# Row maxima of an attention kernel transposed in fp32 and split on GpSimd, and two of four row blocks normalized on ScalarE

## The chip, the cores and the metric

The kernel runs on one core of one Trainium2 chip. The time is the device time of one execution in microseconds, and the time given is the median of the runs. A profiled execution has two figures: its own time, as the runs have it, and its span, from the first to the last instruction of the program.

## The reference, cut to what matters

One transformer block over S = 2048 rows of width D = 512. A condition vector gives six modulation rows. The first half is attention with 32 heads of width 16 that share one key and one value head; the second half is a gated feed-forward layer with F = 1792.

```python
def _A_ref(x, wq, wk, wv, wo):
    q = (x @ wq).reshape(B, S, H, Dh).transpose(0, 2, 1, 3)
    k = x @ wk
    v = x @ wv
    scores = einsum("bhqd,bkd->bhqk", q, k) * (Dh ** -0.5)
    p = softmax(scores, axis=-1)
    o = einsum("bhqk,bkd->bhqd", p, v)
    return o.transpose(0, 2, 1, 3).reshape(B, S, H * Dh) @ wo

def _B_ref(x, w_gate, w_up, w_down):
    return (sigmoid(x @ w_gate) * (x @ w_up)) @ w_down

sa, ca, ga, sb, cb, gb = (silu(c) @ w_mod).reshape(6, -1)
h = layernorm(x) * (1 + ca) + sa
x = x + ga * _A_ref(h, ...)
h = layernorm(x) * (1 + cb) + sb
x = x + gb * _B_ref(h, ...)
```

The weights are drawn large, so the scores are large, and softmax needs the maximum of each row before the exponential is taken.

## The kernel before, in words

**Maxima first, then scores.** The rows are cut into 4 blocks of 512, and a block's 32 heads into 8 units of 4 heads: 32 units in all. For a unit the kernel computes its scores twice. First with queries on the partitions: a matmul writes 128 queries by 512 keys into a PSUM bank (`sa`), and VectorE takes the maximum of each row out of it (`mx`, one TENSOR_REDUCE a bank, 64 banks a unit, 2048 in all). Then with keys on the partitions (`st`): ScalarE takes the exponential (`P`), and TensorE multiplies it with the values (`c`). The products are fp16 with high and low parts in the contraction; P, V and their product are fp32.

**How the maximum gets into the scores.** The second product subtracts the maximum by itself: the query tile `qp` (fp16, 64 rows of contraction for each of two row groups) has two rows that hold the maximum divided by 16, its high and its low fp16 part, and the key tile `kp` has -16 there. So after a unit's 64 maxima `max_end` (line 547) reduces them to `m16` (128x16), makes the two parts on VectorE (`mhl`), and `max_rows` (line 555) turns them on TensorE with an fp16 identity into a PSUM bank of the `sa` rotation, ScalarE copies that to `mh`, and SyncE's queue issues four small DMAs that put the rows into `qp` (line 564). The first `st` of the unit waits for these DMAs.

**The main loop** (line 968) has 512 steps, 16 a unit. A step issues four `st` with their exponentials, four `sa` with their maxima, which run `A0` banks ahead of the step's own unit, and the value product of two steps ago. Blocks 1 to 3 carry in the same steps, in pieces between the score matmuls, the output projection and the feed-forward layer of the block before (`po`, `pgu`, `pd`); block 0 carries the queries' projection of later blocks (`pq`). With A0 = 80 the last maxima of unit i fall into step 16i-5, `max_end` and `max_rows` into step 16i-4; the unit's first `st` is in step 16i. From step 492 on no maxima are left. The last block's output projection and feed-forward layer follow the loop.

**What sets the order.** TensorE, VectorE and ScalarE run in the order in which the code is written (`Ordered`, line 122) up to the end of the loop; GpSimd's and SyncE's instructions outside `pool1` and `sp1` are put in order by the scheduler's own clock. Each engine's queue runs strictly in that order. Ahead of the loop the order is written out by hand in `PLAN` (line 36), a string of tokens: S statistics of a 128-row tile, ra rb rc the inverse deviation (VectorE, GpSimd, VectorE), N the normalization of a tile (`ln_norm`, line 389), T the transposes of a block, H E L the high part, full value and low part of the modulated rows, pk KB KL the keys, pv V the values, q QA QL the queries' projection, pm me pr m the modulation, `a` one `sa` matmul, `x` its maximum, mx and my `max_end` and `max_rows` of unit 0. `PLAN` has A0 tokens `a`. Beside this GpSimd splits the weights into fp16 parts during block 0 (`wst`, `gw`, `wdh`, `wdl`).

Of the kernel before, what the change touches and what calls it, by code (L numbers as in the profile page):

```python
# [8 lines left out]
F16 = mybir.dt.float16  # L9
F32 = mybir.dt.float32  # L10
AF = mybir.ActivationFunctionType
ALU = mybir.AluOpType
# [4 lines left out]
P = 128  # L17
# [14 lines left out]
SM = 16.0  # L32
# [1 line left out]


PLAN = (
# [12 lines left out]
)  # L49

H32 = ('ADAD', 'AAAA', 'AAAA', 'AAAA')
HLO = ('PDPD', 'PPPP', 'PPPP', 'PPPP')

A0 = 80
LAG = 2


# [21 lines left out]
def adaln_mqa_glu_kernel(  # L79
# [15 lines left out]
    pool, sp = nc.gpsimd, nc.sync  # L95
# [3 lines left out]
    x = x[0]  # L99
    out = out[0]  # L100

    cp = ctx.enter_context(tc.tile_pool(name="cp", bufs=1))
    wp = ctx.enter_context(tc.tile_pool(name="wp", bufs=1))
# [11 lines left out]
    def sbank(name):  # L115
        return psum["s"].tile([P, 512], F32, tag=name, name=name, bufs=psum["banks"][name])
# [14 lines left out]
    pe, dve, act = Ordered(nc.tensor), Ordered(nc.vector), Ordered(nc.scalar)  # L131
# [51 lines left out]

    ident = cp.tile([P, P], F32, name="ident")
    make_identity(nc, ident)
    ident16 = cp.tile([P, P], F16, name="ident16")
    pool.tensor_scalar(ident16, ident, 1.0, 0.0, op0=ALU.mult, op1=ALU.add)
    mhalf = cp.tile([P, 1], F32, name="mhalf")
    pool.memset(mhalf, -0.5)

# [169 lines left out]
    def xs(b):  # L360
        return [xall[:, 4 * b + t, :] for t in range(4)]
# [21 lines left out]
    def ln_newton(b):  # L383
        mv, ve, rs, nw = lns[b]
        dve.tensor_tensor(nw, rs, rs, op=ALU.mult)
        dve.scalar_tensor_tensor(nw, nw, -0.5, ve, op0=ALU.mult, op1=ALU.mult)
        dve.scalar_tensor_tensor(rs, nw, 1.5, rs, op0=ALU.add, op1=ALU.mult)

    def ln_norm(b, t):
        mv, ve, rs, nw = lns[b]  # L390
        dve.tensor_scalar(xs(b)[t], xs(b)[t], mv[:, t, 0:1], rs[:, t:t + 1], op0=ALU.subtract, op1=ALU.mult)

    def ln1_tr(b, k):
        pts[b, k] = pt = bank("pt")
# [120 lines left out]
    def get_q(i):  # L515
        b, u = units[i]
        o = u // 2
        if (b, o) not in qps:
            assert (b, o) in qdone
            load_q(b, o)  # L520
        return qps[b, o], 2 * (u % 2)
# [24 lines left out]

    def max_end(i):
        m16 = wp.tile([P, 16], F32, tag="m16", name="m16", bufs=4)
        mhl = wp.tile([P, 2, 16], F16, tag="mhl", name="mhl", bufs=4)
        dve.tensor_reduce(m16.rearrange("p (h t) -> p h t", t=4), mxs[i], axis=AX.X, op=ALU.max)  # L550
        dve.tensor_scalar(mhl[:, 0], m16, 1.0 / SM, None, op0=ALU.mult)
        dve.scalar_tensor_tensor(mhl[:, 1], m16, 1.0 / SM, mhl[:, 0], op0=ALU.mult, op1=ALU.subtract)
        return lambda: max_rows(i, mhl)

    def max_rows(i, mhl):
        qp, pr0 = get_q(i)
        pm = sbank("sa")
        pe.matmul(pm[:32, :P], mhl.rearrange("p h m -> p (h m)"), ident16, start=True, stop=True)
        mh = wp.tile([32, P], F16, tag="mh", name="mh", bufs=4)
        act.activation(mh, pm[:32, :P], AF.Identity)  # L560
        for j in range(2):
            for h in range(2):
                r = 64 * j + 48 + h
                sp.dma_start(qp[r:r + 1, pr0:pr0 + 2, :], mh[16 * h + 8 * j:16 * h + 8 * j + 8, :])


    def st_tile(i, t, pr, j):
# [287 lines left out]
    def q_end(b, o):  # L855
# [3 lines left out]
    blanks.append(blank(pool1))  # L859

    stages = {"S": ln_stats, "ra": ln_eps, "rb": ln_pow, "rc": ln_newton, "N": ln_norm, "T": ln1_tr, "H": ln1_high,
              "E": ln1_full, "L": ln1_low, "pk": k_product, "KB": k_high, "KL": k_end, "pv": v_product, "V": v_end,
              "wh": wq_high, "wl": wq_low, "q": q_part, "QA": q_end, "QL": lambda b, o: q_low(b, o, *q2s.pop((b, o))),
              "pm": mod_product, "me": mod_copy, "pr": mod_sum, "m": mod_end,
              "a": a_next, "x": lambda: a_max(*held.pop(0)), "mx": lambda: rows.append(max_end(0)), "my": lambda: rows.pop()(),
              "lw": load_wq, "lx": load_x, "lm": lambda i: load_mod(i, sp1), "bl": lambda: blanks.append(blank(pool1))}
    for tok in PLAN.split():
        name = tok.rstrip("0123456789")
        stages[name](*[int(z) for z in tok[len(name):]])
    assert not held and apos == A0  # L870
    first.clear()
# [18 lines left out]
    nw, wdone = len(wjobs), 0  # L890
# [77 lines left out]
    for i, (b, u) in enumerate(units):  # L968
# [4 lines left out]
        for kb in range(NKB):  # L973
# [3 lines left out]
            for z in [z for z in waits if z[0] <= s]:  # L977
                waits.remove(z)
                z[1]()
            rows = [max_end(*z) for z in late]  # L980
            an = A0 + 4 * s

# [88 lines left out]
```

## Time and profile before

| what | value |
|---|---|
| median of 3 runs (lowest to highest) | 1727.74 us (1721.31 to 1727.91) |
| the profiled execution's own time | 1730.16 us |
| its span | 1728.4 us |
| first `st` of the loop, from the span's start | 104.62 us |
| first `st` of unit 8 (block 1) | 438.72 us |
| last exponential's score matmul | 1579.99 us |

How it is read: times are in microseconds from the span's start. PE is TensorE's matmuls, PEld its weight loads, DVE VectorE, ACT ScalarE, POOL GpSimd, SP SyncE, whose queue issues the DMAs. A row of a timeline gives the start, the duration, the engine, the line, the operation, what it writes and reads, how many were merged, and in brackets how long the engine had been idle before it and what ended that. A row of windows gives for a stretch the busy time of each engine and the granted TensorE clock (1.00 is full). A row of the chain gives the start and the time that one link holds on the path that ended last. Most matmuls are listed under the line of a helper (L128).

### The profile page before, as it was taken

Reading aid. Unit: us, or ns where it says so; the run is one execution under the profiler, and the core shown is the slowest. Engines: PE = TensorE matmul, PEld = TensorE weight load, DVE = VectorE, ACT = ScalarE, POOL = GpSimd, SP = SyncE. Lnnn points to the kernel's source line nnn. Section 1 sums busy time; section 2 is a strip of 40 time slices with the busy share of each in tenths; the row PEclk is TensorE's granted clock in tenths of the full one; section 3 lists DMA queues with packets and bytes.
Section 4 is the critical chain, followed back from the end, with each engine's and each line's share of the span. In section 5 each row is a group of like instructions: output and inputs, shape, how many; then the busy total and the mean of one; then the engine's idle time right before and its main releaser. Section 6 shows DMA issues by size and latency. Waiting matters only on the chain.

```text
span 1728.4 us, 34828 instructions
## 1 busy us (share of the span) xinstructions
PE 1690.8 (98%) x13968; PEld 576.7 (33%) x13968; DVE 1441.5 (83%) x2424; ACT 1234.2 (71%) x2254; POOL 590.7 (34%) x659
## 2 busy tenths in 40 slices
PE   6999999999999999999999999999999999999998
PEld 3323323333333333333323333333333333323443
DVE  8899999999998998998899898898898888932311
ACT  4358888888888777777778777777778777774100
POOL 4341453542454131332254231223254130231533
PEclk9999999999999999999999999999999999999999
DMA  7121322320101010111011110111001110011211
GB/s 241 45 89 35 118 89 75 129 80 23 58 23 45 30 50 11 38 47 35 24 41 32 41 57 5 33 41 50 32 28 46 32 54 5 30 50 55 76 59 49
DMA packets 66282, 90.88 MB, mean 53 GB/s; under 512 B 14800, under 2 KB 41424, under 8 KB 66120
## 3 DMA queue, kind: packets, MB, share of 16 engines
q1 hardware_dynamic: 66120, 88.66, 16.2%
q8 instruction: 109, 1.79, 0.4%
q14 instruction: 53, 0.43, 0.1%
HBM read 67.68 MB, written 16.22 MB: 49 GB/s over the span
## 4 chain that ended last, share of the span: by engine, by line
PE 81%; DVE 14%; ACT 2%; issue 1%; DMA 1%; POOL 0%; SPq 0%; POOLq 0%; DVEq 0%; ACTq 0%
PE c L128 25%; PE st L128 19%; PE pgu L128 12%; DVE mx L128 11%; PE sa L128 8%; PE pd L128 5%; PE pgu L152 4%; PE pd L152 2%; ACT P L128 2%; PE po L128 2%; PE pq L128 2%; PE pt L128 1%; DVE st L128 1%; DMA xall<-in_A_x_dram 1%; PE po L152 1%
## 5 line engine op out<-in xcount | busy, mean ns | idle before, releaser
L128 DVE TENSOR_REDUCE mx<-sa 128x1 f32<-128x512 f32 x2048 | 1288.1, 684 | 113.6 <-PE sa L128 107.1
L128 ACT ACTIVATE P<-st 128x512 f32<-128x512 f32 x2048 | 1136.6, 596 | 288.3 <-PE sa L128 246.5
L128 PE MATMUL sa<-kp,qp 64*128 64x512 f16 x2048 | 748.2, 383 | 6.8 <-DVE mx L128 6.2
L128 PE MATMUL st<-qp,kp 64*128 64x512 f16 x2048 | 747.6, 380 | 5.9 <-ACT P L128 2.5
L128 PE MATMUL c<-P,V 128*32 128x512 f32 (+1 forms) x5296 | 577.9, 509 | 0.9 <-ACT cs L128 0.2
L128 PEld LDWEIGHTS <-kp 64*128 64x128 f16 x2048 | 177.2, 94 | 516.5 <-issue 427.9
L128 PE MATMUL pgu<-h2h,gw 64*128 64x512 f16 x1344 | 247.1, 376 | 0.3 <-DVE ot L128 0.2
L128 PEld LDWEIGHTS <-qp 64*128 64x128 f16 x2048 | 186.8, 93 | 167.8 <-issue 77.3
L128 PEld LDWEIGHTS c<-P,V 128*32 128x32 f32 x5296 | 104.5, 108 | 191.4 <-issue 182.5
L791 POOL TENSOR_SCALAR th<-th 128x512 f32<-128x512 f32 x42 | 25.9, 617 | 384.1 <-ACT th L128 384.1
L128 PE MATMUL pgu<-h2l,gw 64*128 64x512 f16 x672 | 134.7, 376 | 0.0
L128 PEld LDWEIGHTS <-gw 64*128 64x128 f16 x2016 | 101.0, 94 | 84.5 <-issue 7.4
L501 POOL MEMSET qp<- 32x2048 f16 x28 | 50.3, 1798 | 64.3 <-issue 32.1
L814 POOL TENSOR_TENSOR ot<-ot,gb 128x512 f32<-128x512 f32 x10 | 12.7, 1269 | 168.8 <-ACT ot L128 168.8
L152 PE MATMUL pgu<-h2h,gw 128*128 128x512 f16 x224 | 67.0, 379 | 1.2 <-POOL h2h L307 1.2
L276 POOL TENSOR_SCALAR wst<-wst 128x512 f32<-128x512 f32 x46 | 28.4, 618 | 114.0 <-DMA wst<-in_B_w_gate_dram 57.4
L797 POOL TENSOR_TENSOR gl<-th,gh 128x512 f16<-128x512 f32 x56 | 64.8, 1157 | 4.7
L785 ACT ACTIVATE th<-pgu 128x512 f32<-128x512 f32 x14 | 8.4, 597 | 79.3 <-PE pgu L152 79.3
L794 DVE SCALAR_TENSOR_TENSOR th<-th,pgu 128x512 f32<-128x512 f32 x14 | 9.6, 688 | 66.0 <-PE pgu L152 51.9
L128 DVE COPY u<-pgu 128x512 f32<-128x512 f32 x42 | 28.5, 680 | 37.9 <-PE st L128 22.0
L654 POOL TENSOR_TENSOR raw<-raw,rb 128x512 f32<-128x512 f32 x15 | 19.1, 1274 | 105.3 <-DMA rb<-lD 73.2
L792 POOL TENSOR_TENSOR th<-th,u 128x512 f32<-128x512 f32 x42 | 53.3, 1268 | 5.3 <-DVE u L128 2.3
(156 smaller groups left out, 1304.6 us busy)
## 6 DMA issues: line engine op xcount, KB each, us to landing
gw<-wD SPq DMA_DIRECT2D x56, 512.0 KB
wD<-gw SPq DMA_DIRECT2D x14, 512.0 KB
wm<-in_w_mod_dram SPq DMA_DIRECT2D x6, 1024.0 KB
qp<-qD SPq DMA_DIRECT2D x96, 64.0 KB
qD<-q SPq DMA_DIRECT2D x16, 256.0 KB
raw<-cs SPq DMA_DIRECT2D x128, 32.0 KB
xr<-in_A_x_dram SPq DMA_DIRECT2D x16, 256.0 KB
out_dram<-ot SPq DMA_DIRECT2D x16, 256.0 KB
```

What stands on the lines that cost most here:

```text
L128: return (lambda *a, **k: keep(f_(*a, **k))) if pinned else f_
L152: pe.matmul(self.bank, l_, r_, start=(n == 0), stop=(n == self.n - 1))
L276: pool.tensor_scalar(w_, w_, SW, 0.0, op0=ALU.mult, op1=ALU.add)
L501: eng.memset(qp[j:j + 32], 0.0)
L654: keep(pool.tensor_tensor(raw, raw, rb, op=ALU.mult))
L785: act.activation(th, p_, AF.Tanh, scale=0.5 / (SH * SW))
L791: pool.tensor_scalar(th, th, 1.0, 1.0, op0=ALU.add, op1=ALU.mult)
L792: pool.tensor_tensor(th, th, u_, op=ALU.mult)
L794: dve.scalar_tensor_tensor(th, th, 1.0, p_, op0=ALU.add, op1=ALU.mult)
L797: pool.tensor_tensor(lo, th, hi, op=ALU.subtract)
L814: pool.tensor_tensor(ot, ot, mods[5], op=ALU.mult)
```

## The change

Three things are edited, and the written order is made anew.

- **Maxima.** `max_end` makes `m16` alone. `max_rows` turns `m16` (fp32, 128x16) with the fp32 identity, ScalarE copies the result, scaled by 1/16, to `m32` (16x128, fp32), and GpSimd makes the high part (TENSOR_SCALAR) and the low part (TENSOR_TENSOR) in `mh` (16x2x128, fp16). These two and the four DMAs are put into the scheduler's order with priority. The fp16 identity is gone.
- **Normalization.** For blocks 2 and 3 of the rows `ln_newton` makes -mean times the inverse deviation as well (one more VectorE instruction of 128x4), and the eight tiles are normalized by ScalarE's ACTIVATE with scale and bias in place of VectorE's TENSOR_SCALAR.
- **Lead.** A0 goes from 80 to 84: `max_end` of unit i falls into step 16i-5, and no maxima are left from step 491 on.

```diff
@@ PLAN: two of its lines, before and after @@
-    'S12 wl0 T01 S13 T02 m0 E01 H00 T03 ra1 E00 S20 rb1 H01 E03 H02 S21 L00 E02 L01 q000 H03 rc1 L02 N10 q001 L03 '
+    'T00 m0 S12 T01 H00 S13 E00 T02 E01 H01 L00 T03 ra1 S20 H02 E02 L01 rb1 q000 H03 E03 pk00 L02 rc1 q001 L03 pk01 '
...
-    'q113 x a x a QA11 x a x a QL11 x a x x x '
+    'q101 x QL03 a q102 x a x q103 x a a QA10 q110 x a q111 x QL10 a x a q112 mx x a my q113 x a x QA11 a x a x a '
+    'QL11 x a x a x a x a x a x a x a x a x a x a x a x a x x x '
@@
-A0 = 80
+A0 = 84
@@
-    ident16 = cp.tile([P, P], F16, name="ident16")
-    pool.tensor_scalar(ident16, ident, 1.0, 0.0, op0=ALU.mult, op1=ALU.add)
@@ ln_newton
+        if b > 1:
+            dve.scalar_tensor_tensor(nw, mv[:, :, 0], -1.0, rs, op0=ALU.mult, op1=ALU.mult)
@@ ln_norm
-        dve.tensor_scalar(xs(b)[t], xs(b)[t], mv[:, t, 0:1], rs[:, t:t + 1], op0=ALU.subtract, op1=ALU.mult)
+        if b < 2:
+            dve.tensor_scalar(xs(b)[t], xs(b)[t], mv[:, t, 0:1], rs[:, t:t + 1], op0=ALU.subtract, op1=ALU.mult)
+        else:
+            act.activation(xs(b)[t], xs(b)[t], AF.Identity, scale=rs[:, t:t + 1], bias=nw[:, t:t + 1])
@@ max_end
-        mhl = wp.tile([P, 2, 16], F16, tag="mhl", name="mhl", bufs=4)
         dve.tensor_reduce(m16.rearrange("p (h t) -> p h t", t=4), mxs[i], axis=AX.X, op=ALU.max)
-        dve.tensor_scalar(mhl[:, 0], m16, 1.0 / SM, None, op0=ALU.mult)
-        dve.scalar_tensor_tensor(mhl[:, 1], m16, 1.0 / SM, mhl[:, 0], op0=ALU.mult, op1=ALU.subtract)
-        return lambda: max_rows(i, mhl)
+        return lambda: max_rows(i, m16)
@@ max_rows
-        pe.matmul(pm[:32, :P], mhl.rearrange("p h m -> p (h m)"), ident16, start=True, stop=True)
-        mh = wp.tile([32, P], F16, tag="mh", name="mh", bufs=4)
-        act.activation(mh, pm[:32, :P], AF.Identity)
-        for j in range(2):
-            for h in range(2):
-                r = 64 * j + 48 + h
-                sp.dma_start(qp[r:r + 1, pr0:pr0 + 2, :], mh[16 * h + 8 * j:16 * h + 8 * j + 8, :])
+        pe.matmul(pm[:16, :P], m16, ident, start=True, stop=True)
+        m32 = wp.tile([16, P], F32, tag="m32", name="m32", bufs=4)
+        act.activation(m32, pm[:16, :P], AF.Identity, scale=1.0 / SM)
+        mh = wp.tile([16, 2, P], F16, tag="mh", name="mh", bufs=4)
+        with tc.high_priority():
+            pool.tensor_scalar(mh[:, 0], m32, 1.0, 0.0, op0=ALU.mult, op1=ALU.add)
+            pool.tensor_tensor(mh[:, 1], m32, mh[:, 0], op=ALU.subtract)
+            for j in range(2):
+                for h in range(2):
+                    r = 64 * j + 48 + h
+                    sp.dma_start(qp[r:r + 1, pr0:pr0 + 2, :], mh[8 * j:8 * j + 8, h, :])
```

VectorE ahead of the loop, from the statistics of the last tiles to its first maxima (`xall` is the row tile that is normalized in place, `nw` and `rs` the steps to the inverse deviation, `kp` the keys). Before:

```order
L128 TENSOR_TENSOR nw<-rs 128x4
L128 SCALAR_TENSOR_TENSOR nw<-nw,ve 128x4
L128 SCALAR_TENSOR_TENSOR rs<-nw,rs 128x4
L128 TENSOR_REDUCE mx<-sa 128x1 x4
L128 TENSOR_SCALAR xall<-xall,mv,rs 128x512 x4
L128 SCALAR_TENSOR_TENSOR kp<-pk,kh 128x512
L128 TENSOR_REDUCE mx<-sa 128x1 x8
```

After:

```order
L128 TENSOR_TENSOR nw<-rs 128x4
L128 SCALAR_TENSOR_TENSOR nw<-nw,ve 128x4
L128 SCALAR_TENSOR_TENSOR rs<-nw,rs 128x4
L128 SCALAR_TENSOR_TENSOR nw<-mv,rs 128x4
L128 TENSOR_REDUCE mx<-sa 128x1 x4
L128 SCALAR_TENSOR_TENSOR kp<-pk,kh 128x512
L128 TENSOR_REDUCE mx<-sa 128x1 x11
```

The four normalizations of block 3 have left VectorE (those of block 2, a little earlier, as well), and one small instruction has come. On ScalarE seven of the eight now stand in a row:

```order
L128 ACTIVATE h1h_436<-pt,sa,ca 128x512
L128 ACTIVATE h_439<-pt,sa,ca 128x512
L128 ACTIVATE xall<-xall,nw,rs 128x512 x7
L128 ACTIVATE h1h_502<-pt,sa,ca 128x512
L128 ACTIVATE kh<-pk,kbias,kscale 128x512
```

They stand between the rows of block 1 (`h1h`, `h`) and those of block 2, where before the first followed on the second.

SyncE's queue in block 0, around the rows of unit 5 (`qD` is the queries' way through memory, `wst` a weight tile that comes in, `wD` one that goes out, `raw` and `lD` the end of a unit). Before:

```order
L483 DMA qD<-q_4178 128x2x512
L275 DMA wst<-in_B_w_up_dram 128x4x128
L483 DMA qD<-q_4184 128x2x512
L564 DMA qp<-mh 1x8x128 x4
L683 DMA wD<-gw 128x2048
```

After:

```order
L486 DMA qD<-q_4202 128x2x512
L568 DMA qp<-mh 1x8x128 x4
L273 DMA wst<-in_B_w_up_dram 128x4x128
L486 DMA qD<-q_4208 128x2x512
L687 DMA wD<-gw 128x2048
```

The four small DMAs now stand ahead of one weight load and one store of queries.

More of the change, by code (lines that the diff above doesn't have):

```diff
@@ L548, in max_end, with max_rows @@
         m16 = wp.tile([P, 16], F32, tag="m16", name="m16", bufs=4)
-        mhl = wp.tile([P, 2, 16], F16, tag="mhl", name="mhl", bufs=4)
         dve.tensor_reduce(m16.rearrange("p (h t) -> p h t", t=4), mxs[i], axis=AX.X, op=ALU.max)
-        dve.tensor_scalar(mhl[:, 0], m16, 1.0 / SM, None, op0=ALU.mult)
-        dve.scalar_tensor_tensor(mhl[:, 1], m16, 1.0 / SM, mhl[:, 0], op0=ALU.mult, op1=ALU.subtract)
-        return lambda: max_rows(i, mhl)
-    def max_rows(i, mhl):
+        return lambda: max_rows(i, m16)
+    def max_rows(i, m16):
         qp, pr0 = get_q(i)
         pm = sbank("sa")
-        pe.matmul(pm[:32, :P], mhl.rearrange("p h m -> p (h m)"), ident16, start=True, stop=True)
-        mh = wp.tile([32, P], F16, tag="mh", name="mh", bufs=4)
-        act.activation(mh, pm[:32, :P], AF.Identity)
-        for j in range(2):
-            for h in range(2):
-                r = 64 * j + 48 + h
-                sp.dma_start(qp[r:r + 1, pr0:pr0 + 2, :], mh[16 * h + 8 * j:16 * h + 8 * j + 8, :])
+        pe.matmul(pm[:16, :P], m16, ident, start=True, stop=True)
[9 more added lines that the diff above has]
+                    sp.dma_start(qp[r:r + 1, pr0:pr0 + 2, :], mh[8 * j:8 * j + 8, h, :])
     def st_tile(i, t, pr, j):
```

19 rows, old and new, of the table PLAN are left out of this document.

## The prediction

> **What bounds the kernel now.** I read first the totals, then the windows of three stages, then the chain and the timelines inside them. Totals and windows (columns of the latter: stretch, its length, busy time of PE, PEld, DVE, ACT, POOL with instruction counts, granted clock, DMA share, GB/s):
>
> ```profile
> PE 1690.8 (98%) x13968; PEld 576.7 (33%) x13968; DVE 1441.5 (83%) x2424; ACT 1234.2 (71%) x2254; POOL 590.7 (34%) x659
> ```
>
> ```profile
> 0.00:104.62 104.62, 85.12 (x541) 35.83 (x542) 91.02 (x173) 41.95 (x68) 39.83 (x52) 0.93 0.41 135
> 105.00:438.70 333.70, 325.76 (x3287) 103.34 (x3284) 324.61 (x543) 288.08 (x537) 139.93 (x166) 0.98 0.25 80
> 527.70:1488.20 960.50, 959.08 (x7990) 318.28 (x7988) 865.54 (x1438) 745.20 (x1359) 291.84 (x307) 1.00 0.12 35
> 104.62:112.30 7.68, 6.11 (x29) 1.76 (x30) 7.68 (x14) 5.48 (x10) 6.72 (x10) 0.66 0.62 202
> ```
>
> The average (PE 98%) hides three stages. Ahead of the loop DVE works 91.02 of 104.62 us. In block 0 (105 to 438.7) it works 324.61 of 333.70 and idles 9.1; PE's 325.76 is as much, but there PE's in-order queue stands behind DVE's, as the next fence shows. In blocks 1 to 3 PE is full (959.08 of 960.50) and DVE has a tenth free. So an instruction taken from DVE is worth its length ahead of the loop and in block 0, and little later.
>
> **Edit 1, normalization on ScalarE.** The chain ahead of the loop (start, time on the path, link), from two stretches of it:
>
> ```profile
> 35.65 2.76 DVE xall L128 x4
> ...
> 42.81 1.08 DVE rs L128
> ...
> 46.29 3.50 DVE xall L128 x4
> ...
> 101.27 0.32 PE sa L128 x2
> 101.59 0.75 PE pq L128 x3
> ```
>
> Up to 50 us the path runs through DVE, and the eight normalizations of blocks 2 and 3 are links of it: 2.76 + 3.50 = 6.3 us go. Two instructions of 128x4 come (`nw` from mean and inverse deviation). Their nearest row is the link `rs`, 1.08, beside a busy GpSimd; the same kind of work took a fifth of that elsewhere, as the 128x16 instructions below do. I take 0.6 each, 1.2 (ends 0.3 and 2.2). ScalarE takes eight ACTIVATEs; the nearest is
>
> ```profile
> 52.65 0.78 ACT L128 ACTIVATE h1h<-pt,sa,ca 128x512 f16<-128x512 f32 x1 [3.33 <-PE pt L128]
> ```
>
> 0.78 each, 6.2 us at most. ScalarE is busy 41.95 of these 104.62 us, and just there it waits 3.33 us for transposes: that is the cover, so nothing is added. If it fails, block 2's transposes come late by up to the seven in a row, 5.5 us, and the gain is gone.
>
> **Edit 2, four more maxima ahead of the loop.** Four reductions at 0.6 are 2.4 us of DVE more here. They buy nothing by their number (each step of block 0 still has four) but give the rows of a unit one step more to arrive. On the path PE holds the later part (0.75 for three `pq`, 0.32 for one or two `sa`), so four `sa` cost at most 1.3 there, inside DVE's 2.4.
>
> Unit 0's `mhl` pair goes too, 0.3. Sum ahead of the loop: -6.3 + 1.2 + 2.4 - 0.3 = **-3.0**. Ends: -6 (the four reductions fill gaps that DVE has anyhow) and +2.4 (PE holds the start and DVE's gain is lost).
>
> The last lines of the new plan are `x a` pairs with nothing else on PE: DVE paces them, and PE is mostly idle. The window 104.62 to 112.30 shows what that does now: granted clock 0.66, but DVE busy 7.68 of 7.68, so it cost nothing there. I take 0, ends 0 and +2. The Trainium skill's page "TensorE: Matmul & The Clock Gate" (What's actually happening) says that the array falls to half its clock after an idle window of about 3.4 us and recovers after a busy one. By that rule the longer tail would start the loop cold for longer, and the sum would be 2 us higher.
>
> **Edit 3, the maxima's two parts off DVE: block 0.** DVE around unit 1's `max_end`, then unit 3's:
>
> ```profile
> 124.76 12.35 DVE L128 TENSOR_REDUCE mx<-sa 128x1 f32<-128x512 f32 x20
> 137.14 0.22 DVE L128 TENSOR_REDUCE m<-mx 128x16 f32<-128x64 f32 x1
> 137.40 0.17 DVE L128 TENSOR_SCALAR mhl<-m 128x16 f16<-128x16 f32 x1
> 137.60 0.18 DVE L128 SCALAR_TENSOR_TENSOR mhl<-m,mhl 128x16 f16<-128x16 f32 x1
> 137.70 2.48 DVE L128 TENSOR_REDUCE mx<-sa 128x1 f32<-128x512 f32 x4
> 140.37 7.52 DVE L128 TENSOR_REDUCE mx<-sa 128x1 f32<-128x512 f32 x12 [0.19 <-PE sa L128]
> ```
>
> ```profile
> 219.31 0.98 DVE L128 TENSOR_SCALAR mhl<-m 128x16 f16<-128x16 f32 x1
> 220.33 0.54 DVE L128 SCALAR_TENSOR_TENSOR mhl<-m,mhl 128x16 f16<-128x16 f32 x1
> 220.80 2.47 DVE L128 TENSOR_REDUCE mx<-sa 128x1 f32<-128x512 f32 x4
> 223.60 0.69 DVE L128 TENSOR_REDUCE mx<-sa 128x1 f32<-128x512 f32 x1 [0.33 <-PE sa L128]
> ...
> 226.01 7.67 DVE L128 TENSOR_REDUCE mx<-sa 128x1 f32<-128x512 f32 x12 [0.86 <-PE sa L128]
> ```
>
> A step is 4 x 12.35 / 20 = 2.47 us, all DVE. `max_end` holds the next maximum from 137.14 to 137.70; without `mhl` it would start at 137.40, 0.30 sooner. The 0.19 of idle time behind is the PE that could turn only what `mhl` had finished; it goes too. 0.49 for each of the eight units 1 to 8 that block 0 prepares: -3.9. Unit 3's pair took 1.49 to the next maximum where 0.30 is usual, and 0.33 + 0.86 of idle time followed: 1.2 + 1.0 more, -2.2.
>
> The rows' DMAs are late once, at unit 5 (SP's queue, DVE behind it, and the link of the last DMA in the chain):
>
> ```profile
> 311.88 0.36 SPq L483 DMA_DIRECT2D qD<-q  x1
> 312.29 2.71 SPq L564 DMA_DIRECT2D qp<-mh  x4
> ```
>
> ```profile
> 315.28 0.69 DVE L128 TENSOR_REDUCE mx<-sa 128x1 f32<-128x512 f32 x1 [0.89 <-PE sa L128]
> 316.55 0.69 DVE L128 TENSOR_REDUCE mx<-sa 128x1 f32<-128x512 f32 x1 [0.58 <-PE sa L128]
> ```
>
> ```profile
> 314.36 1.68 DMA qp<-mh
> ```
>
> They stood behind a store of queries; the new order has them ahead of it. Of 0.89 + 0.58 I count -1.0.
>
> Against this stands the longer way of the rows. For unit 1 the queue issued them from 138.39:
>
> ```profile
> 138.39 2.71 SPq L564 DMA_DIRECT2D qp<-mh  x4
> ```
>
> so `m` to the last issue takes 1.25 + 2.1, and 1.68 to its landing: 5.0 us of the four steps, 9.9, that stand between `m` and the unit's first scores. New are two GpSimd instructions of 128 elements. Their nearest rows are one of a single element and the 512-element subtractions:
>
> ```profile
> L295 POOL TENSOR_TENSOR nw<-nw,ve x10: 189/190/190, 501.9 to 1277.0; 128x1 f32<-128x1 f32 x10
> ```
>
> ```profile
> 387.21 0.22 DVE L128 TENSOR_REDUCE m<-mx 128x16 f32<-128x64 f32 x1
> ```
>
> ```profile
> 391.98 2.27 POOL L278 TENSOR_TENSOR wdl<-wst,wdh 128x512 f16<-128x512 f32 x2
> ```
>
> 0.19 and 1.13 each; a quarter of the way gives some 0.4, with the hand-over 0.9 for both (ends 0.5 and 2.4). The five steps of the new lead are 12.3, so 12.3 - 5.9 = 6.4 us remain for GpSimd's queue. In the new order the `wdl` pair stands ahead of unit 7's two instructions, and it ended at 394.25. Unit 7's `m`, one step sooner, is at 384.7; its rows would land at 394.25 + 0.9 + 2.1 + 1.68 = 398.9, 1.8 behind 387.21 + 9.9. I count +1.0 for this one unit; elsewhere the queue is clear by then. Block 0: -3.9 - 2.2 - 1.0 + 1.0 = **-6.1**, ends -9.1 (all of DVE's idle time) and +3.
>
> **Edit 3 in blocks 1 to 3.** PE around unit 20's turn of the maxima:
>
> ```profile
> 994.67 1.07 PE L128 MATMUL c<-P,V 128*32 128x512 f32 x8
> 995.55 0.22 PE L128 MATMUL sa<-ident,mhl 128*32 128x128 f16 x1
> 995.70 0.39 PE L128 MATMUL st<-qp,kp 64*128 64x512 f16 x1
> 995.86 0.37 PE L128 MATMUL sa<-kp,qp 64*128 64x512 f16 x1
> ...
> 998.11 1.06 PE L128 MATMUL c<-P,V 128*32 128x512 f32 x8
> 999.11 0.39 PE L128 MATMUL st<-qp,kp 64*128 64x512 f16 x1
> 999.11 0.39 PE L128 MATMUL sa<-kp,qp 64*128 64x512 f16 x1
> ```
>
> After `c` the next `st` and `sa` start together 1.00 later; here 1.03 and 1.19. In fp32, `c` needs 1.00 for 512 columns, so 128 need 0.25 where the fp16 turn held PE for 0.15: +0.1, with a slower weight load +0.2. Against it `sa` was 0.16 late because its bank waited for DVE, which is now 0.30 sooner. Over the 23 units 9 to 31: +2.3 to +4.6 and -3.7; I take **0**, ends -4 and +5. The ACTIVATE out of the bank stays one instruction for one.
>
> **Sum.** -3.0 - 6.1 = -9.1 against the profiled execution's own 1730.2 (span 1728.4): 1721. That execution is 2.4 above the median of the runs, 1727.7; from the median it would be 1718.6. I say 1719.
>
> **Rivals.**
> *The rows come too late (slower).* GpSimd's queue is in order; if what the new order puts ahead of the two instructions waits for a weight load, the first scores of a unit wait, and PE with them. For: GpSimd is busy 139.93 us of block 0, and unit 7 is already over the line. Against: 6.4 us of room, and priority in the order. It decides where the queue holds a unit by more than 6.4 us: three us beyond that at each of the eight units of block 0 cost 24, so 1721 - 7 + 24 = 1738, or 1736 from the median. The Trainium skill speaks for it on its page "GPSIMD Engine Reference" (When to use GPSIMD): elementwise work belongs on VectorE, since GpSimd is about twice as slow with two inputs. No row here shows the 16x128 form.
> *It nets out (no change).* PE holds the start of the loop (+1 ahead of it), block 0 gains only the 0.30 for eight units (-2.4), and the fp32 turn costs its 0.2 for 23 units (+4.6): +3, so 1733 and 1731 from the median. For: the chain after 50 us is PE's. Against: the 0.19 and 0.86 of idle time behind `mhl`.
> *All of it.* Both lower ends, -6 and -9, and -2 later: 1713 and 1711 from the median.
>
> **How the numbers follow.** 0.6 for the forecast (1714 to 1724), 0.22 for no net change, 0.12 for late rows, 0.06 for all of it. The range 1710 to 1730 leaves out the late rows and the upper half of the second. Half a per cent, 8.6 us, is about what a measurement of this kernel tells from no change: below 1719.1 is faster. The forecast lies on that edge. I put 0.42 of its 0.6 below it, because the idle time of DVE that I left out of block 0 (9.1 us in all, of which the rows above use 4) can only shrink, and add all of the last case: 0.48. Slower is the late rows, 0.12; the rest is 0.40.
>
> **What would show it.** Right: the first `st` near 101.6 though 84 maxima are made; `m` directly followed by `mx` and 0.26 between them at all units; unit 8's first `st` near 429.6; steps with `max_rows` in blocks 1 to 3 as long as before. Wrong: ScalarE the longest link between 30 and 55 us; PE or its weight loads waiting for `qp` rows at more than one or two units; GpSimd's two instructions starting many us after ScalarE's copy; a granted clock of half beyond 115 us; a first `st` at 105 or later.

## The result and the profile after

The changed kernel takes 1717.72 us (median), and the kernel before 1726.49 in the six runs that belong to this result (1727.74 is the median of the first three of them): the ratio is 0.9952, with a 95% interval of 0.9939 to 0.9965. Against further runs of the kernel before on another occasion it was 0.9942 (0.9924 to 0.9960). The profile below is of an execution from that second occasion, because the first one that was profiled was disturbed (4015.82 us, where the others took 1716.82 to 1718.80).

Totals of the changed kernel, then windows of its three stages (columns as in the prediction's windows): ahead of the first `st`, block 0 up to unit 8's first `st`, and units 8 to 30:

```profile
PE 1680.2 (98%) x14000; PEld 577.0 (34%) x14000; DVE 1421.9 (83%) x2354; ACT 1237.8 (72%) x2262; POOL 613.1 (36%) x722
```

```profile
0.00:100.71 100.71, 82.71 (x546) 36.15 (x547) 85.33 (x169) 47.16 (x76) 43.91 (x58) 0.97 0.45 151
100.71:428.11 327.40, 320.93 (x3299) 104.26 (x3298) 320.76 (x527) 287.00 (x537) 142.17 (x178) 0.99 0.24 78
428.11:1520.76 1092.65, 1090.48 (x9156) 360.11 (x9153) 974.44 (x1589) 855.43 (x1564) 363.88 (x422) 1.00 0.11 35
```

The last two of these stages in the kernel before:

```profile
104.62:438.72 334.10, 326.16 (x3289) 103.54 (x3289) 325.01 (x543) 288.10 (x537) 140.33 (x166) 0.98 0.25 80
438.72:1535.00 1096.28, 1093.45 (x9137) 360.95 (x9134) 984.17 (x1639) 855.95 (x1564) 347.52 (x377) 1.00 0.12 35
```

All three stages became shorter: by 3.9 us ahead of the loop, 6.7 in block 0 and 3.6 in units 8 to 30, 14.2 in all. That is more than the medians differ, since these two executions lie on opposite sides of their medians. The table has the same split for every kernel below; the last stage (unit 31 and the tail) is 193.4 us in all of them. The stages are differences of `st` start times. Two executions of the kernel before differ by 1.54 us in the first column, 0.99 in block 0 and 0.22 in units 8 to 30; the last section shows where the first two come from.

| kernel | first `st` | block 0 | units 8 to 30 | median | ratio to before (95%) |
|---|---|---|---|---|---|
| before | 104.62 | 334.10 | 1096.28 | 1727.74 | |
| before, another execution | 103.08 | 333.11 | 1096.06 | 1727.43 (one run) | |
| after | 100.71 | 327.40 | 1092.65 | 1717.89 | 0.9942 (0.9924 to 0.9960) |
| before + edit of the maxima | 104.95 | 333.36 | 1093.42 | 1727.05 | 0.9986 (0.9973 to 0.9999) |
| before + ScalarE normalization | 105.34 | 335.20 | 1096.08 | 1728.64 | 1.0000 (0.9989 to 1.0012) |
| before + early projections | 105.09 | 332.60 | 1096.19 | 1729.84 | 1.0019 (1.0009 to 1.0029) |
| after, old way of the maxima | 102.34 | 330.31 | 1095.17 | 1722.82 | 0.9969 (0.9958 to 0.9981) |
| the same, fp16 turn twice | 102.29 | 331.33 | 1095.59 | 1723.26 | 0.9972 (0.9962 to 0.9982) |
| after, normalization on VectorE | 101.05 | 328.09 | 1092.64 | 1717.80 | 0.9944 (0.9927 to 0.9962) |
| after, 80 maxima ahead | 98.41 | 334.84 | 1093.44 | 1721.99 | 0.9970 (0.9957 to 0.9982) |
| after, late projections | 105.53 | 328.72 | 1092.77 | 1721.56 | 0.9965 (0.9951 to 0.9979) |
| after, fp32 turn twice | 102.62 | 327.60 | 1097.55 | 1722.95 | 0.9973 (0.9961 to 0.9984) |
| after, units 2 and 7 old way | 102.68 | 328.07 | 1092.72 | 1717.98 | 0.9940 (0.9926 to 0.9954) |

### The profile page after: what moved, and what is told of

Read it like the earlier page. It is cut to its first block, busy times and chain, and to the rows that moved or that the text cites. A ratio compares the mean times of both kernels' runs of the same rounds, so it can differ in the third digit from the quotient of the medians.

```text
span 4014.0 us, 34893 instructions
## 1 busy us (share of the span) xinstructions
PE 3996.8 (100%) x14000; PEld 798.1 (20%) x14000; DVE 1537.6 (38%) x2354; ACT 1334.3 (33%) x2262; POOL 612.6 (15%) x722
## 4 chain that ended last, share of the span: by engine, by line
PE 99%; issue 0%; DVE 0%; DMA 0%; ACT 0%; POOL 0%; SPq 0%; POOLq 0%; DVEq 0%
PE c L128 30%; PE st L128 16%; PE pgu L128 15%; PE sa L128 14%; PE pd L128 6%; PE pgu L152 5%; PE pd L152 3%; PE pq L128 3%; PE po L128 2%; PE pt L128 1%; PE po L152 1%; PE pk L128 1%; PE pmod L128 0%; PE prow L128 0%; DVE mx L128 0%
## 5 line engine op out<-in xcount | busy, mean ns | idle before, releaser
L128 DVE TENSOR_REDUCE mx<-sa 128x1 f32<-128x512 f32 x2048 | 1393.2, 691 | 1915.9 <-PE sa L128 1455.9
L128 PE MATMUL st<-qp,kp 64*128 64x512 f16 x2048 | 1510.1, 770 | 0.2
L128 PE MATMUL sa<-kp,qp 64*128 64x512 f16 x2048 | 1490.3, 768 | 1.0 <-DVE mx L128 0.8
L128 PE MATMUL c<-P,V 128*32 128x512 f32 (+1 forms) x5296 | 1270.2, 1060 | 0.0
L128 PE MATMUL pgu<-h2h,gw 64*128 64x512 f16 x1344 | 546.9, 830 | 0.0
L128 PE MATMUL pgu<-h2l,gw 64*128 64x512 f16 x672 | 294.5, 832 | 0.0
L128 PE MATMUL pd<-wdh,gl 64*128 64x512 f16 x280 | 118.6, 836 | 0.0
L128 PE MATMUL pd<-wdl,gh 64*128 64x512 f16 x280 | 117.5, 832 | 0.0
L128 PE MATMUL pd<-wdh,gh 64*128 64x512 f16 x280 | 117.2, 830 | 0.0
L152 PE MATMUL pgu<-h2l,gw 128*128 128x512 f16 x112 | 93.6, 836 | 0.0
```

Source lines behind the costliest of these rows:

```text
L128: return (lambda *a, **k: keep(f_(*a, **k))) if pinned else f_
L152: pe.matmul(self.bank, l_, r_, start=(n == 0), stop=(n == self.n - 1))
```

## Experiments

My theory was that of the prediction: VectorE's time ahead of the loop and in block 0 pays, blocks 1 to 3 give nothing. The rivals: PE holds the start of the loop whatever VectorE does; the rows' longer way makes PE wait; the gain lies later than I put it.

### The changed kernel and the kernel before, once more

Edit: none.

> The changed kernel once more, to have a profile that can be set beside the one before. My theory (gain ahead of the loop and in block 0, nothing later): first st near 101.6, unit 8's first st near 429.6, blocks 1 to 3 as long as before, ratio 0.995. Rival A (PE holds the start of the loop): first st at 104 to 106, and block 0 shorter by 8 us or more. Rival B (the gain is in blocks 1 to 3, where max_end frees the banks sooner): first st and unit 8 less than 3 us sooner, the rest shorter by 4 us or more.

> The kernel before once more, for a second profile: how far two executions of the same kernel differ by stage. First st within 1.5 us of 104.62, block 0 within 2 us of 334.1, the rest within 1.5 us of 1289.7.

Measured: the rows and the table above. The first `st` and unit 8 stand near where the theory has them (100.71 and 428.11), and yet units 8 to 30 are 3.6 us shorter, which it excluded. Rival B named that place, but it also forecast less than 3 us in the stages ahead, which gained 10.6. The two executions of the kernel before differ by 0.22 us in units 8 to 30, and no execution has a granted clock under 1.00 there, so these 3.6 are no chance. The first `st` of the second execution, 1.54 sooner, lies just outside the 1.5 expected.

### One edit alone: ScalarE normalization, in the old order and out of the new

```diff
@@ ln_newton and ln_norm, into the kernel before @@
+        if b > 1:
+            dve.scalar_tensor_tensor(nw, mv[:, :, 0], -1.0, rs, op0=ALU.mult, op1=ALU.mult)
...
+        if b < 2:
+            dve.tensor_scalar(xs(b)[t], ...)
+        else:
+            act.activation(xs(b)[t], xs(b)[t], AF.Identity, scale=rs[:, t:t + 1], bias=nw[:, t:t + 1])
```

> The kernel before with the normalization of blocks 2 and 3 on ScalarE and nothing else, in the old order. By the prediction's term (-6.3 + 1.2): first st near 99.5, some 1722 where before has 1727. Rival (PE's own sequence from 52 us on holds the start, whoever normalizes): first st within 1 us of 104.6, ratio 0.999 to 1.001.

The same lines taken out of the changed kernel, whose order stays:

```diff
-        if b > 1:
-            dve.scalar_tensor_tensor(nw, mv[:, :, 0], -1.0, rs, op0=ALU.mult, op1=ALU.mult)
...
-        if b < 2:
+        if True:
             dve.tensor_scalar(xs(b)[t], ...)
```

> The changed kernel with the normalization of blocks 2 and 3 back on VectorE, in the new order's places, without the -mean/deviation instructions. My theory: +6.3 - 1.2 = +5.1 us ahead of the loop against the changed kernel, first st near 107, some 1723. Rival (PE's chain holds the start of the loop and VectorE has gaps there): first st within 1 us of the changed kernel's, time within 1 us.

Measured: 1728.64 against 1728.47 (ratio 1.0000), and 1717.80 where the changed kernel has 1717.89. No gain shows in either order, and the interval of the first (0.9989 to 1.0012) excludes the 5 us expected. The chains ahead of the loop say why. With ScalarE normalizing in the old order (start, time on the path, link):

```profile
34.05 0.81 ACT xall L128
...
45.70 0.81 ACT xall L128
46.51 0.67 ACT h L128
47.18 0.71 ACT xall L128
47.89 0.67 ACT kh L128
48.55 1.41 ACT xall L128 x2
49.96 0.67 ACT h1h L128
```

In the changed kernel:

```profile
40.40 2.22 ACT xall L128 x3
42.62 0.67 ACT h1h L128
```

And with the normalization back on VectorE in the new order:

```profile
40.32 0.91 DVE xall L128 x2
41.23 0.60 DVE mx L128
41.83 0.46 DVE xall L128
```

The path does not leave the normalization; it follows it to the other engine, where one tile takes 0.7 to 0.8 of the path (on VectorE 0.46 in the new order; in the old one 2.76 and 3.50 for four tiles, so as much), and the high parts of the rows (`h1h`, `h`) queue behind it. PE got no more done for it: between 20 and 54 us it is busy 24.6 us with ScalarE normalizing in the old order and 24.9 without, and from 54 us on it is full in both. So the rival's numbers came true, and its reason too: PE's work from there on holds the start of the loop, and the edit did not bring it forward.

### The edit of the maxima alone, and taken out

Into the kernel before go `max_end` and `max_rows` of the change's diff, whole; `PLAN`, A0 = 80 and `ln_norm` stay:

```diff
-        dve.tensor_scalar(mhl[:, 0], m16, 1.0 / SM, None, op0=ALU.mult)
-        dve.scalar_tensor_tensor(mhl[:, 1], m16, 1.0 / SM, mhl[:, 0], op0=ALU.mult, op1=ALU.subtract)
...
+        with tc.high_priority():
+            pool.tensor_scalar(mh[:, 0], m32, 1.0, 0.0, op0=ALU.mult, op1=ALU.add)
+            pool.tensor_tensor(mh[:, 1], m32, mh[:, 0], op=ALU.subtract)
...
```

> The kernel before with the edit of the maxima alone (fp32 turn, two parts on GpSimd, priority), old order, 80 maxima ahead, all normalization on VectorE. My theory: -0.3 ahead of the loop, -6.1 in block 0, 0 later: ratio 0.9963, some 1720 where before has 1726.5. Rival A (the rows' longer way needs the fifth step: with four only 4.0 us are left for GpSimd's queue): first scores wait for qp rows at several units of block 0, ratio 1.000 or above. Rival B (the parts were free on VectorE): ratio 0.999 to 1.001 without waits.

The reverse in the changed kernel: both parts on VectorE and the fp16 turn, while the new order, 84 ahead and ScalarE normalization stay:

```diff
+        dve.tensor_scalar(mhl[:, 0], m16, 1.0 / SM, None, op0=ALU.mult)
+        dve.scalar_tensor_tensor(mhl[:, 1], m16, 1.0 / SM, mhl[:, 0], op0=ALU.mult, op1=ALU.subtract)
...
-            pool.tensor_scalar(mh[:, 0], m32, 1.0, 0.0, op0=ALU.mult, op1=ALU.add)
-            pool.tensor_tensor(mh[:, 1], m32, mh[:, 0], op=ALU.subtract)
...
```

> The changed kernel with the old way of the maxima (both parts on VectorE, fp16 turn, no priority), the new order, 84 ahead and the normalization on ScalarE kept. My theory: -2.7 ahead of the loop, -1.0 in block 0 (unit 5's rows no longer late): ratio 0.9979, some 1723. Rival (the whole gain is ahead of the loop and of the longer lead): ratio 0.995, first st no later than in the changed kernel.

Measured: alone it gives 0.9986, so 2 us and not 6; taken out of the changed kernel it costs 4.9 us (1722.82 against 1717.89). In units 8 to 30 it is worth about as much in both, 2.9 and 2.5 us, but at different units (shown in the section on the prediction). The difference is block 0: with four steps between `m` and the first scores, units 2, 5 and 7 wait for `qp` rows (unit 5 alone loses some 6 us, its last step ahead and first two at 5.41, 4.83 and 3.11 in place of 2.45, the last two of them largely at a granted clock of 0.50), which eats the VectorE time saved. The edit of the maxima needs the longer lead; what the lead is worth without that edit was not run.

### Four maxima fewer ahead

```diff
@@ in the changed kernel @@
-    'QL11 x a x a x a x a x a x a x a x a x a x a x a x a x x x '
+    'QL11 x a x a x a x a x a x a x a x a x x x '
...
-A0 = 84
+A0 = 80
```

> The changed kernel with 80 maxima ahead: the last four pairs of a matmul and its maximum leave the written order, the first scores of a unit come four steps after its m in place of five. Theory A (the fifth step is what keeps GpSimd's pair harmless): first st 2.4 us sooner than in the changed kernel, at 98.3, but block 0 longer by some 6 us, since GpSimd's or SyncE's queue makes units 2, 5 and 7 wait for qp rows as in the run of the maxima's edit alone; some 1721. Theory B (the rows have time either way): first st 2.4 sooner, block 0 as long, 1715.5.

Measured: first `st` at 98.41, that is 2.30 sooner, and block 0 at 334.84, 7.4 longer (1.0 of it in the first three steps, where this execution has half the clock for longer; the medians, 4.1 apart, agree with some 6.4). Theory A. A weight load of unit 5 in this kernel (idle time before it, and what ended it), and GpSimd's queue ahead of its pair, whose maxima ScalarE had copied at 296.88:

```profile
308.29 0.09 PEld L128 LDWEIGHTS <-kp 64*128 64x128 f16 x1 [3.50 <-DMA qp<-mh]
```

```profile
301.50 0.62 POOL L274 TENSOR_SCALAR wst<-wst 128x512 f32<-128x512 f32 x1 [1.00 <-DMA wst<-in_B_w_up_dram]
302.20 1.16 POOL L485 TENSOR_TENSOR q<-q,q 128x512 f16<-128x512 f32 x1
303.32 0.62 POOL L275 TENSOR_SCALAR gw<-wst 128x512 f16<-128x512 f32 x1
304.02 1.16 POOL L276 TENSOR_TENSOR gw<-wst,gw 128x512 f16<-128x512 f32 x1
305.15 0.29 POOL L563 TENSOR_SCALAR mh<-m 16x128 f16<-16x128 f32 x1
```

The pair stood 8.3 us behind the splitting of weights and queries, part of it waiting for a weight load, and the room with four steps is smaller than that. In the changed kernel the same pair stood only 3.6 us (294.60 to 298.16), so the lead changed the queue ahead of it as well as the room.

### The price of a turn

```diff
@@ max_rows, in the changed kernel @@
         pe.matmul(pm[:16, :P], m16, ident, start=True, stop=True)
+        pe.matmul(pm[:16, :P], m16, ident, start=True, stop=True)
```

> The changed kernel with the fp32 turn of the maxima issued twice into the same bank, which measures the turn's price: its two passes and two weight loads. Theory A (blocks 1 to 3 are full on PE, and each turn costs its length there): +0.2 to +0.3 for each of 23 units, +4.6 to +7 in all, nothing in block 0; some 1723. Theory B (PE waits at that place for the bank anyhow, so a turn costs less than 0.1): +0 to +2.

The same with the fp16 turn, in the changed kernel with the old way of the maxima:

```diff
         pe.matmul(pm[:32, :P], mhl.rearrange("p h m -> p (h m)"), ident16, start=True, stop=True)
+        pe.matmul(pm[:32, :P], mhl.rearrange("p h m -> p (h m)"), ident16, start=True, stop=True)
```

> The changed kernel with the old way of the maxima, and its fp16 turn issued twice: the price of the turn that the change replaced, to set beside 0.21 us for an fp32 turn (units 8 to 30 took 4.90 us more with it issued twice). Against the run without the second turn (units 8 to 30: 1095.17). Theory A (PE's time, 0.15 each): +3.4 in these units, so that the fp32 form cost only 0.06 a unit more. Theory B (an fp16 turn is nearly free): +1 or less, and the fp32 turn costs its whole 0.2.

Measured: units 8 to 30 take 4.90 us more with a second fp32 turn, 0.21 a unit (at every unit but one), and block 0 takes 0.2 more. A second fp16 turn costs those units 0.42 us in all, 0.02 each: theory B. The turns as matmuls (the second row is of the kernel with the old way; two passes each in fp32, hence 64):

```profile
L128 PE MATMUL sa<-ident,m 128*16 128x128 f32 x64 | 12.2, 273 | 0.3 <-DVE m L128 0.3
```

```profile
L128 PE MATMUL sa<-ident,mhl 128*32 128x128 f16 x32 | 7.1, 223 | 3.1 <-DVE mhl L128 3.1
```

Two things make the second fp16 turn so cheap. It is short by itself: at eight of the 23 turns it costs 0.05 to 0.12. At the others it costs next to nothing, which fits steps that VectorE holds (the fp16 turn even waits 3.1 us in all for `mhl`), where PE has time to spare; step by step this was not separated. In the changed kernel PE bounds the step, and an fp32 turn costs its 0.21.

### The order of the projections

Which part of the new order moves the start of the loop? It has four projections of queries (`q010` to `q013`) and the first value product (`pv0`) ahead of 54 us. They go back behind `V3`, and in the mirror image into the early part of the old order:

```diff
@@ PLAN of the changed kernel @@
-    ... ra3 pv0 L11 H13 E13 rb3 pk10 V0 N20 pk11 N21 L12 rc3 q010 N22 a ... KB1 a a E20 x a a q011 KL1 ...
+    ... ra3 L11 H13 E13 rb3 pk10 N20 pk11 N21 L12 rc3 N22 a ... KB1 a a E20 x a a KL1 ...
-    ... x x x a a a q020 V3 x a q021 ...
+    ... x x x a a a V3 q010 x a q011 x a q012 x a q013 x a QA01 q020 x a q021 ...
-    ... E33 a pv1 x L33 bl x pk32 x pk33 V1 a KB3 a a x a pv2 ...
+    ... E33 a pv0 x L33 bl x pk32 V0 x pk33 a KB3 pv1 a a x a V1 pv2 ...
@@ PLAN of the kernel before @@
-    ... S33 H12 T20 L11 ra3 E12 a ... L12 rc3 H20 ... a a L21 a KL1 a E22 x pk20 H23 L22 x pk21 E23 x a a T30 ...
+    ... S33 H12 T20 pv0 L11 ra3 E12 V0 a ... L12 rc3 q010 H20 ... a a q011 L21 a KL1 q012 a E22 x pk20 H23 L22 x pk21 q013 E23 x a a QA01 T30 ...
-    ... V3 q010 x a q011 x a x a q012 x a q013 x a x a QA01 q020 ...
+    ... V3 x a x a x a x a x a x a q020 ...
```

> The changed kernel with one piece of its new order undone: the four projections q010 to q013 (three matmuls each) and the first value product pv0, which the new order has ahead of 54 us, back at the late places of the old order. Theory A (the gain ahead of the loop is PE work moved out of the stretch from 54 us on, which PE bounds): 4 x (1.075 - 0.60) + 1.3 = +3.2 us, first st near 104, some 1721. Theory B (other parts of the order do it): first st within 0.7 of the changed kernel's two looks, 100.7 to 102.6, time within 1 us of 1717.9.

> The mirror of it: the kernel before with only these tokens moved early in its order, everything else as it was (normalization and both parts of the maxima on VectorE, 80 ahead). Theory A: -3.2 us, first st near 100.5, some 1725. If the early stretch has no free PE time in the old order, or VectorE bounds it (19.29 of 20 us busy from 20 to 40 us): 0, first st 103 to 105.

Measured: late in the new order, 1721.56, 3.7 us more than the changed kernel; first `st` at 105.53, 3.0 behind executions of the new order that have a half-clock spell at the same stage, as this one has (102.3 to 102.7). Theory A. Early in the old order there is no gain, 1729.84. The reason seems to lie in what my edit left behind: six pairs of one maximum and one matmul with nothing else for PE, in the middle of PE's stretch. Windows of four us there, and the links of the chain in the second:

```profile
80.00:84.00 4.00, 2.97 (x29) 1.02 (x26) 3.89 (x8) 0.00 (x0) 0.00 (x0) 0.84 0.02 4
84.00:88.00 4.00, 3.99 (x9) 0.77 (x8) 3.04 (x5) 0.00 (x0) 0.00 (x0) 0.50 0.00 0
```

```profile
84.59 1.40 PE pq L128 x3
...
86.53 1.40 PE pq L128 x3
```

PE idles a quarter of the first window, and the granted clock is 0.50 from 82.72 us on, for 6.8 us: two groups of projections at 1.40 in place of 0.75, and one `sa` behind each at 0.54 in place of 0.32. By my estimate that is 2 to 3 us, the size of the gain expected; that the idling brought the half clock on is likely, but not shown. So this run doesn't settle what the early places alone are worth in the old order.

### Units 2 and 7 the old way

```diff
@@ max_end, in the changed kernel @@
+        if i not in (2, 7):
+            return lambda: max_rows(i, m16)
+        ... mhl on VectorE as before ...
+        return lambda: max_rows16(i, mhl)
```

> The changed kernel with the old way of the maxima for units 2 and 7 alone, the two whose rows GpSimd's queue holds for some 8 us. If those two waits are GpSimd's queue (1.18 us at unit 2, 0.25 + 0.90 at unit 7): both go, VectorE pays 2 x 0.42: -1.5 us in block 0, 325.9, some 1716.4. If SyncE's queue or the transfer holds them: the first steps stay late and block 0 is 328 or more.

Measured: 1717.98 (the changed kernel has 1717.89); no gain shows. Block 0 reads 328.07, but its first three steps took 10.76 in this execution and 9.48 in the changed kernel's, by a longer stretch at half the clock; behind them it is 0.6 shorter, so the 328 of the expectation decides nothing. Unit 7's wait is gone, but VectorE's first part took 0.73 there instead of 0.17, and the step 3.98 where the changed kernel has 2.99. Unit 2's rows still come late, by 0.35 in place of 1.18, now by SyncE's queue (the rows were ready in `mh` at 175.49):

```profile
181.07 2.56 SPq L706 DMA_DIRECT2D wD<-gw  x2
183.73 2.76 SPq L572 DMA_DIRECT2D qp<-mh  x4
```

Ahead of the rows stands a store of split weights, and that waits for GpSimd. So taking the pair off GpSimd does not free unit 2's rows. In the kernel before they stood behind the same store (the store at 182.55, the rows at 185.21) and yet came in time.

## Why the prediction came out where it did

Forecast 1719, measured 1717.72 to 1717.89. The total is right, but for the first stage that is luck: the gain counted there does not exist, and another that I did not see stands in its place. A second one that I did not see lies in blocks 1 to 3.

| step | predicted | measured |
|---|---|---|
| normalization off VectorE, net | -6.3 + 1.2 = -5.1 | 0 (1728.64 to 1728.47; 1717.80 to 1717.89) |
| the rest of the new order | only the tail was priced | -4.7 (first `st` at 98.41 with 80 ahead, against 103.08; against 104.62 it would be -6.2, but that execution has a half-clock spell at 73 us that the other two lack) |
| four more maxima | +2.4 | +2.3 (98.41 to 100.71) |
| tail of pairs, cold start | 0 (0 to +2) | -0.3 here (first three steps 9.79 before, 9.48 after), up to +1.1 in other executions of the new order (last section) |
| block 0: `mhl` pair, unit 3 | -3.9 - 2.2 | -4.9, and -1.5 that is the clock's (below) |
| unit 5's rows | -1.0 | -1.9 |
| unit 7's rows | +1.0 | +1.15 |
| unit 2's rows | not counted | +1.2 |
| blocks 1 to 3 | 0 (-4 to +5) | -3.6: -2.5 to -2.9 the maxima's edit, the rest the lead |

**Normalization: wrong.** The step that failed is "ScalarE is busy 41.95 of these 104.62 us, and just there it waits 3.33 us for transposes: that is the cover, so nothing is added". The wait was real, but it does not lie where the tiles had to go: in the kernel before ScalarE works without a gap from 43.36 to 49.33 (rows, keys and weights), and only then waits. In the changed kernel its work became the path: the sign named in the prediction, ScalarE the longest link between 30 and 55 us, is what the chain after shows (2.22 us of three tiles at 40.40). What is written there for a failing cover, "and the gain is gone", is what happened. That the start of the loop came sooner all the same is the order's doing: PE is busy 28.3 us between 20 and 54 us, 24.9 before, and its last projection ends at 92.9. What follows is VectorE's alone:

```profile
92.94 0.37 PE sa L128 x2
93.31 7.85 DVE mx L128 x13
```

In the kernel before PE's chain went on to 103.8. The projections and the value product are 3.0 to 3.7 us of the 4.7; which tokens give the rest stays open. The prediction read the new order for VectorE's rows and did not ask which PE work had moved ahead of the stretch that PE bounds.

**Block 0: right in kind, one term too large.** VectorE around `max_end` of units 1 and 3:

```profile
130.50 0.22 DVE L128 TENSOR_REDUCE m<-mx 128x16 f32<-128x64 f32 x1
130.64 10.78 DVE L128 TENSOR_REDUCE mx<-sa 128x1 f32<-128x512 f32 x17
```

```profile
212.30 0.22 DVE L128 TENSOR_REDUCE m<-mx 128x16 f32<-128x64 f32 x1
212.44 10.18 DVE L128 TENSOR_REDUCE mx<-sa 128x1 f32<-128x512 f32 x16
```

The next maximum follows at once, with no idle time behind. The eight steps that hold `m` took, by the starts of their `st`, 3.42, 3.53, 4.59, 3.42, 3.16, 3.42, 3.68 and 3.42, and the one behind the third 3.96; now 3.01, 2.79, 2.99 and five between 2.99 and 3.00. The eight give 4.87 us (4.5 against the other execution of the kernel before). The 3.96 is another matter: that step lies in a half-clock spell from 223.12 to 226.53, and the other execution, with unit 3's pair just as long (0.44 and 1.09) but no spell there, has 2.45 in its place. So the "0.33 + 0.86 of idle time" that the prediction put to unit 3's pair, 1.0 us of its -2.2, came for the most part from the clock; PE's idling during the pair (busy 2.95 of 4.00 us from 218 to 222, in both) may have brought the spell on, but not every time. Unit 5's wait is gone (two steps of 3.51 and 3.26 before, 2.45 each now).

**The rows' way: right in size, one unit missed.** GpSimd's two instructions:

```profile
L564 POOL TENSOR_TENSOR mh<-m,mh 16x128 f16<-16x128 f32 x32 | 13.4, 419 | 2.5
L563 POOL TENSOR_SCALAR mh<-m 16x128 f16<-16x128 f32 x32 | 9.3, 290 | 142.5 <-ACT m L128 142.2
```

From ScalarE's copy to the end of both it is 0.88 (92.49 to 93.37); I had 0.9. Their queue at units 7 and 2, and PE's weight loads that waited:

```profile
381.33 2.27 POOL L276 TENSOR_TENSOR wdl<-wst,wdh 128x512 f16<-128x512 f32 x2
383.57 0.29 POOL L563 TENSOR_SCALAR mh<-m 16x128 f16<-16x128 f32 x1
```

```profile
387.82 0.09 PEld L128 LDWEIGHTS <-kp 64*128 64x128 f16 x1 [1.21 <-DMA qp<-mh]
```

```profile
176.86 3.39 POOL L276 TENSOR_TENSOR gw<-wst,gw 128x512 f16<-128x512 f32 x3
180.22 0.29 POOL L563 TENSOR_SCALAR mh<-m 16x128 f16<-16x128 f32 x1
```

```profile
184.30 0.09 PEld L128 LDWEIGHTS <-kp 64*128 64x128 f16 x1 [1.57 <-DMA qp<-mh]
```

Unit 2 was held 7.8 us (172.43 to 180.22) and its scores were 1.2 late (a step of 3.63), unit 3 was held 4.9 and not late, unit 7 8.1 and 1.15 late (2.70 and 3.35). If lateness is what exceeds the room, the room is between 6.6 and 7.0 us; the prediction had 6.4. "Elsewhere the queue is clear by then" failed at unit 2. The rival of late rows was the same mechanism with a threshold that two units cross by a little; with the lead at four steps, unit 5 crosses its smaller one by far.

The Trainium skill's "GPSIMD Engine Reference" (When to use GPSIMD), which keeps elementwise work on VectorE, goes the other way here: the two instructions take 0.29 and 0.42 on GpSimd where VectorE, undisturbed, had 0.17 and 0.18, and yet the edit that moves them is worth 4.9 us in the new order: VectorE paces block 0, and two pairs behind it would be held up beside GpSimd.

**Blocks 1 to 3: inside the ends, off by 3.6.** The step that failed is the weighing of "+2.3 to +4.6" for the turn against "-3.7" for its bank. PE around unit 20's turn after:

```profile
979.96 1.06 PE L128 MATMUL c<-P,V 128*32 128x512 f32 x8
980.84 0.38 PE L128 MATMUL sa<-ident,m 128*16 128x128 f32 x2
981.16 0.39 PE L128 MATMUL st<-qp,kp 64*128 64x512 f16 x1
981.16 0.39 PE L128 MATMUL sa<-kp,qp 64*128 64x512 f16 x1
```

`st` and `sa` start together 1.20 behind `c`, so `sa` lost nothing (1.19 before) and its later waits are gone: the next `sa` stood at 1.79 before and stands at 1.64 (981.60). The prediction read this one turn and multiplied it by 23, but the gain is not here: unit 20's step stood 0.13 us above others with the same pieces before and 0.19 after. It is at eight turns (units 14 to 16, 22 to 24, 27 and 28), whose step also carries another VectorE instruction of 0.68 us. Unit 23's, before:

```profile
1138.62 0.22 DVE L128 TENSOR_REDUCE m<-mx 128x16 f32<-128x64 f32 x1
1138.88 0.17 DVE L128 TENSOR_SCALAR mhl<-m 128x16 f16<-128x16 f32 x1
...
1139.78 0.68 DVE L128 COPY u<-pgu 128x512 f32<-128x512 f32 x1
```

A step of VectorE's maxima (2.47), `max_end` with the pair (0.56) and this instruction (0.60 to the next start) make some 3.6 us. These steps took 3.66 to 3.83, and others with the same pieces 2.88 to 3.26: VectorE bounds them, and there the edit in the old order gains 0.2 to 0.4 each, together its whole 2.9. Of the other turns unit 18's gains 0.56, and each of the rest gains or loses 0.16 at most. Over all 23 the excess fell from 9.0 to 6.0 us, 0.26 a turn, most of it the turn itself, 0.21. The lead does the rest, 0.8 us in units 17 and 21 to 23: one step earlier the turns of units 22 to 24 no longer share their step with the other instruction. So with 84 ahead the pair would have met none of these; taking the edit out of the changed kernel costs 2.5 us for another reason, 2.4 of it in units 24 and 29, where the pair's second part took 1.19 us in place of 0.18 while GpSimd worked on two tiles of 128x512.

## What to carry to other kernels

A link of the critical chain that is moved to an engine with idle time is not gone: ask what stands in that engine's queue between the moved work and the next link, since idle time a few us away covers nothing. A change that rewrites an order must be read on the engine that bounds the next stretch, here PE from 54 us on, and not only on the engine that the edit is about. Where a step is bound by one engine, another's longer instruction costs only what exceeds the bound; and a longer way for data is harmless up to the room that the lead gives, so the two should be changed, and tested, together.

## What the runs showed of the hardware

**Half-clock spells.** Executions of one order with the same lead start the loop up to 2 us apart, and it goes with the granted clock. Stretches (columns as above) of the kernel before, of the changed kernel with the second turn, and of the changed kernel at the same place and at its tail of pairs:

```profile
72.90:76.30 3.40, 3.40 (x17) 0.69 (x20) 2.50 (x6) 0.60 (x1) 0.00 (x0) 0.50 0.00 0
107.10:113.90 6.80, 6.39 (x31) 1.56 (x34) 6.09 (x11) 4.88 (x9) 6.24 (x9) 0.50 0.33 102
```

```profile
69.50:72.90 3.40, 3.40 (x17) 0.60 (x14) 1.69 (x4) 1.14 (x2) 0.00 (x0) 0.50 0.00 0
```

```profile
69.50:72.90 3.40, 3.40 (x20) 0.98 (x18) 3.02 (x6) 1.79 (x3) 0.00 (x0) 1.00 0.00 0
98.10:108.30 10.20, 8.46 (x27) 1.93 (x26) 10.13 (x18) 4.90 (x9) 7.99 (x12) 0.50 0.40 126
```

The spells last 3.4, 6.8 and 10.2 us (13.7 in three executions), and PE is shown busy all through the two at 72.9 and 69.5, and through the 3.4 us ahead of each. An execution of the new order with one near 69 us has its first `st` at 102.3 to 102.7, one without at 100.7 to 101.1; the kernel before 104.62 with it and 103.08 without. The Trainium skill, "TensorE: Matmul & The Clock Gate" (What's actually happening), has free-running windows of about 3.4 us, and these lengths agree with it. Its rule that the half clock follows an idle window does not fit these two, nor the other spells between 64 and 76 us; ahead of every other spell PE idled for a part of the last 3.4 us. Whether an execution gets one there is chance as far as these runs show. The spell around the start of the loop is not: it lasts 3.4 or 6.8 us in the five executions of the old order and 10.2 or 13.7 in the eight of the new one, as the prediction feared of the tail of pairs. Above it costs nothing, because VectorE (10.13 of 10.20 us busy) paces that stretch. In the five executions of the new order in which it reaches 9.9 us or more beyond the first `st`, in place of 7.5 to 7.8, the first three steps take 10.5 to 10.9 in place of 9.4 to 9.6. In the old order with early projections a spell lay where PE paces, and cost 2 to 3 by the estimate above.

**VectorE's small instructions beside GpSimd.** The 128x16 TENSOR_SCALAR took 0.17 as a rule, but 0.98 at unit 3 before and 0.73 at unit 7 in the kernel with units 2 and 7 the old way, both while GpSimd split weights; the 128x16 TENSOR_REDUCE in front of it never took more than 0.22. The Trainium skill's page "SBUF — State Buffer" (Who interferes with whom) has this split: a TENSOR_SCALAR can take the port pair shared with GpSimd, a TENSOR_REDUCE does not. It makes the removed pair dearer than its usual length, which the prediction counted for unit 3 alone.
